# Talking-heads attention and a squared-ReLU FFN: rows loaded four to a partition, scores per head gathered by DMA into tiles of 10 queries by 12 heads, and the normalisation on GpSimd

## The chip, the cores and the metric

The kernel runs on one core of one Trainium2 chip. The metric is the device time of one execution in microseconds (us); less is better. Nanoseconds are marked ns.

In the profile's lines PE is TensorE's matmul, PEld its weight load, DVE is VectorE, ACT is ScalarE, POOL is GpSimd and SP is SyncE. L276 is line 276 of the kernel in question. "Span" is the length of the profiled execution. The "granted clock" (PEclk) is the share of TensorE's full clock that the profile records for a stretch, and a "run" of a transfer is a stretch of consecutive bytes in memory.

## The reference

There are 8 batches, 12 heads, 448 positions and a head size of 64. Scores are mixed across the heads before the softmax and once more after it ("talking heads"), and the attention's output goes through a squared-ReLU FFN (3584 tokens, 768 to 2048 to 768).

```python
scores = q @ k.T / 8                                   # per batch and head, 448 x 448
scores = einsum('bhij,hg->bgij', scores, w_pre)        # 12 heads -> 12 heads
attn   = exp(scores - max(scores))
attn   = attn / (sum(attn) + 1e-9)
attn   = einsum('bhij,hg->bgij', attn, w_post)         # 12 heads -> 12 heads
x      = (attn @ v) as (3584, 768)
h      = maximum(x @ w_in, 0)
out    = (h * h) @ w_out
```

q, k and v are drawn as normal numbers times 0.1, so the scores are small.

The mixing over heads is the awkward part. For each pair of positions it is a 12 by 12 matrix product. In these matmuls the contraction runs over partitions, so the heads have to lie on partitions, beside some queries: a block-diagonal matrix then mixes the heads of several queries in one matmul.

## The kernel before

It works in steps of 32 queries. 32 queries of 12 heads are 384 rows, which is three full tiles of 128 partitions. The 12 heads are split into 8 and 4 so that everything fits 128 partitions. That makes full use of the partitions, but each output tile needs two mix matmuls (heads 0 to 7, then 8 to 11), and the second mix again takes two.

```python
def load_rows(src, b, st, name):          # 128 positions on partitions: 256-byte runs (64 floats)
    ...
    nc.gpsimd.dma_start(out=t[0:n, :, :],
        in_=src[b, :, 128*st:128*st+n, :].rearrange("h s d -> s h d"))

def score_tile(s, t):                     # 3 per step; four 32-column matmuls each
    for r in range(4):
        nc.tensor.matmul(ps[32*r:32*r+32, 0:S], lhsT=ql[b%2][p][:, n, :], rhs=kts[(b, p)][:, :], ...)
    # copied to SBUF by ACT (t < 2) or DVE

def mix_O(s, u):                          # first mix: heads A, then heads B, into one bank
    nc.tensor.matmul(ps[:, 0:S], lhsT=preA[:, 0:128],  rhs=S_sb[(s, u)], start=True,  stop=False)
    nc.tensor.matmul(ps[:, 0:S], lhsT=preBA[u][:, :],  rhs=S_sb[(s, 2)], start=False, stop=True)
    softmax_tile(s, ps, u)
...                                       # (mix_AB and mix_BB do the third tile)
def softmax_tile(s, ps, t):
    nc.scalar.activation(out=e, in_=ps[:, 0:S], func=ACT.Exp, scale=SCALE, accum_out=sm)
    nc.vector.reciprocal(out=rc, in_=sm)
    nc.vector.tensor_scalar(out=d, in0=e, scalar1=rc, scalar2=1.0/S, op0=ALU.mult, op1=ALU.subtract)

def post(s, jb):                          # second mix, which also turns the tile: 3 per step,
    nc.tensor.matmul(ps[:, 0:384], lhsT=D_sb[(s, 2)][:, js], rhs=postBB, ...)
    for u in range(2):
        nc.tensor.matmul(ps[:, 192*u:192*u+192], lhsT=D_sb[(s, u)][:, js], rhs=postA, ...)
    nc.vector.tensor_copy(out=at[...], in_=ps[:, 0:384]...)
...                                       # (post_last does the 64 positions that remain)
```

The matmuls of attention times V (`ot_unit`) and of the FFN (`ffn1_unit`, `ffn2_unit`) are put in between as filler, so that TensorE has work while the softmax of a step runs.

The softmax here doesn't subtract the row's maximum and nothing guards it: scores larger than these inputs give would overflow.

Of the kernel before, what the change touches and what calls it, by code (L numbers as in the profile page):

```python
# [19 lines left out]
CH = 32  # L20
NCH = S // CH
HC = 16
NHC = S // HC
NHALF = 2
CPH = NCH // NHALF
SH = S // NHALF
SCALE = 1.0 / 8.0
ROWS = [128, 128, 128, 64]





# [3 lines left out]
def kernel(  # L37
# [18 lines left out]
    atbp = ctx.enter_context(tc.tile_pool(name="atbp", bufs=1))  # L56
# [7 lines left out]
    vfull = [[consts.tile([P, H, D], BF16, name=f"v{x}_{jb}") for jb in range(3)] for x in range(2)]  # L64

    vlast = [[consts.tile([P, H, D], BF16, name=f"vl{x}_{u}") for u in range(2)] for x in range(2)]

    def load_rows(src, b, st, name):
        n = ROWS[st]
        t = stage.tile([P, H, D], BF16, name=name, tag=name, bufs=4)  # L70
        nc.gpsimd.dma_start(out=t[0:n, :, :], in_=src[b, :, 128 * st:128 * st + n, :].rearrange("h s d -> s h d"))  # L71
        return t

    def load_qk(b):
        ks = [load_rows(k, b, st, "kst") for st in range(4)]
        qs = [load_rows(q, b, st, "qst") for st in range(4)]
        return qs, ks

    def load_v(b):
        x = b % 2  # L80
        for st in range(3):
            nc.gpsimd.dma_start(  # L82
                out=vfull[x][st][:, :, :], in_=v[b, :, 128 * st:128 * st + 128, :].rearrange("h s d -> s h d"))
        for u in range(2):
            nc.gpsimd.dma_start(
                out=vlast[x][u][64 * u:64 * u + 64, :, :], in_=v[b, :, 384:448, :].rearrange("h s d -> s h d"))

# [4 lines left out]
    def wcol(w, name, heads, eng):  # L92
        t = consts.tile([P, H], F32, name=name)
        for j, h in enumerate(heads):
            src = bass.AP(tensor=w.tensor, offset=w[h, 0:1].offset, ap=[[0, HC], [1, H]])
            eng.dma_start(out=t[HC * j:HC * j + HC, 0:H], in_=src)
        return t

    HA, HB = list(range(8)), [8, 9, 10, 11, 8, 9, 10, 11]
    cols = {  # L100
        "preA": wcol(w_pre, "preA_col", HA, nc.sync),
        "preB": wcol(w_pre, "preB_col", HB, nc.scalar),
        "postA": wcol(w_post, "postA_col", HA, nc.sync),
        "postB": wcol(w_post, "postB_col", HB, nc.scalar),
    }
    staged = {0: load_qk(0)}

    ql = [[consts.tile([P, NHC, 32], BF16, name=f"ql{x}_{p}") for p in range(NPAIR)] for x in range(2)]
    for p in range(NPAIR):
        nc.vector.memset(ql[0][p][:, :, :].rearrange("p a b -> p (a b)"), 0.0)  # L110
# [5 lines left out]
    istripe = consts.tile([P, HC], F32, name="istripe")  # L116
    nc.vector.tensor_reduce(out=istripe[:, :], in_=ident[:, :].rearrange("p (r i) -> p i r", i=HC),
                            axis=mybir.AxisListType.X, op=ALU.add)

    def cat(name):  # L120
        t = consts.tile([P, H, HC], BF16, name=name)
        nc.vector.tensor_tensor(out=t[:, :, :], in0=istripe[:, :].unsqueeze(1).to_broadcast([P, H, HC]),
                                in1=cols[name][:, :].unsqueeze(2).to_broadcast([P, H, HC]), op=ALU.mult)
        return t[:, :, :].rearrange("p g i -> p (g i)")

    preA = cat("preA")
    preB = cat("preB")

    preBA = [consts.tile([P, 128], BF16, name=f"preBA{u}") for u in range(2)]
    preBB = consts.tile([P, 128], BF16, name="preBB")  # L130
    nc.vector.memset(preBB[:, :], 0.0)
    for u in range(2):
        hs = slice(64 * u, 64 * u + 64)
        nc.vector.memset(preBA[u][:, :], 0.0)
        nc.vector.tensor_copy(out=preBA[u][hs, :], in_=preB[hs, 0:128])
        nc.vector.tensor_copy(out=preBB[hs, hs], in_=preB[hs, 128:192])
    postA = cat("postA")
    postB = cat("postB")
    postBB = consts.tile([P, 2 * H * HC], BF16, name="postBB")
    nc.vector.memset(postBB[:, :], 0.0)  # L140
    for u in range(2):
        hs = slice(64 * u, 64 * u + 64)
        nc.vector.tensor_copy(out=postBB[hs, 192 * u:192 * u + 192], in_=postB[hs, :])
# [6 lines left out]
    def late_loads():  # L150
        nc.gpsimd.dma_start(out=wpost_bf[:, :], in_=w_post[0:H, 0:H])
        load_v(0)
        staged[1] = load_qk(1)
        for x in range(2):
            for u in range(2):
                nc.gpsimd.memset(vlast[x][u][64 - 64 * u:128 - 64 * u, :, :].rearrange("p a b -> p (a b)"), 0.0)
        for p in range(NPAIR):
            nc.gpsimd.memset(ql[1][p][:, :, :].rearrange("p a b -> p (a b)"), 0.0)
        for c2 in range(NPAIR):
            nc.gpsimd.dma_start(out=w1[c2][:, :], in_=moe_w_in[c2 * 128:(c2 + 1) * 128, 0:DFF])  # L160
        for ft in range(FT):
            nc.gpsimd.dma_start(out=w2[ft][:, :], in_=moe_w_out[ft * 128:(ft + 1) * 128, 0:DMODEL])

    kts, bvecs, xts, h2ts, atbs = {}, {}, {}, {}, {}

# [11 lines left out]
    def transposes(ps, tiles, p):  # L177
        for st in range(4):
            n = ROWS[st]
            nc.tensor.transpose(ps[:, 128 * st:128 * st + n],  # L180
                                tiles[st][0:n, 2 * p:2 * p + 2, :].rearrange("s h d -> s (h d)"), ident[0:n, 0:n])

    def q_unit(b, p):
        ps = bank("qt_ps", BF16)
        transposes(ps, staged[b][0], p)
        for hh in range(2):
            r = slice(64 * hh, 64 * hh + 64)
            nc.vector.tensor_copy(out=ql[b % 2][p][r, :, 16 * hh:16 * hh + 16],
                                  in_=ps[r, 0:S].rearrange("p (n i) -> p n i", i=HC))

    def k_unit(b, p):
        ps = bank("kt_ps", BF16)
        transposes(ps, staged[b][1], p)
        kt_p = work.tile([P, S], BF16, name="kt_p", tag="kt", bufs=2 * NPAIR)
        nc.scalar.copy(out=kt_p[:, :], in_=ps[:, 0:S])
        kts[(b, p)] = kt_p

    def prologue_units(b):
        return [(400, lambda p=p, f=f: f(b, p)) for p in range(NPAIR) for f in (k_unit, q_unit)]

    def bias_unit(b):

        x = b % 2
        ps = bank("vs_ps")
        srcs = vfull[x] + [vlast[x][0]]
        for c2 in range(NPAIR):
            for jb in range(4):
                nc.tensor.matmul(ps[:, c2:c2 + 1], lhsT=srcs[jb][:, 2 * c2:2 * c2 + 2, :].rearrange("s h d -> s (h d)"),
                                 rhs=onescol[:, 0:1], start=(jb == 0), stop=(jb == 3))
        bv = work.tile([P, NPAIR], F32, name="bvec", tag="bvec", bufs=2)  # L210
        nc.vector.tensor_tensor(out=bv[:, :], in0=ps[:, 0:NPAIR], in1=cgblk[:, :], op=ALU.mult)
        bvecs[b] = bv

    def ot_unit(b, half, cp):

        x = b % 2
        at, at3 = atbs[(b, half)]
        ps = bank("ot_ps")
        for y in range(2):
            for jb in range(3):  # L220
                for hh in range(2):
                    g = 4 * cp + 2 * y + hh
                    nc.tensor.matmul(ps[64 * hh:64 * hh + 64, SH * y:SH * y + SH], lhsT=vfull[x][jb][:, g, :],  # L223
                                     rhs=at[:, jb, g, :], start=(y == 0 and jb == 0), stop=False,
                                     skip_group_check=True)
            for u in range(2):
                for hh in range(2):
                    g = 4 * cp + 2 * y + hh
                    dst = ps[64 * hh:64 * hh + 64, SH * y:SH * y + SH].rearrange("p (c u i) -> p u c i", u=2, i=HC)
                    nc.tensor.matmul(dst[:, u, :, :], lhsT=vlast[x][u][:, g, :], rhs=at3[:, g, :], start=False,  # L230
                                     stop=(u == 1), skip_group_check=True)
        for y in range(2):
            c2 = 2 * cp + y
            if (b, c2) not in xts:
                xts[(b, c2)] = ffnp.tile([P, S], BF16, name="xt", tag=f"xt{c2}", bufs=2)
            nc.scalar.activation(out=xts[(b, c2)][:, SH * half:SH * half + SH], in_=ps[:, SH * y:SH * y + SH],  # L236
                                 func=ACT.Identity, bias=bvecs[b][:, c2:c2 + 1], scale=1.0)
# [143 lines left out]
    with tc.manual_schedule(engines={PE}):  # L381
        for _, f in prologue_units(0):
            f()
# [85 lines left out]
```

## Time and profile before

| | before |
|---|---|
| time, median of 2 runs | 793.04 us (792.63 to 793.45) |
| span of the profiled execution | 791.2 us |
| first score matmul | 22.6 us |
| batch 0, first score matmul to that of batch 1 | 66.2 us |
| batch 1, likewise | 95.0 us |
| batches 2 to 6, likewise | 469.4 us, 93.9 each |
| batch 7 and the tail | 138.0 us |

The page of the kernel before, its busy row (busy time, share of the span, instructions), then the busy tenths of PE and its granted clock in 40 slices, the DMA packets, and the chain of work that ended last by engine:

```profile
PE 750.2 (95%) x7586; PEld 428.6 (54%) x7586; DVE 488.6 (62%) x1249; ACT 482.3 (61%) x1337; POOL 243.2 (31%) x271
...
PE   3689899999999999999999999999999999999997
...
PEclk9999999999999999999999999999999999999999
...
DMA packets 149336, 35.85 MB, mean 45 GB/s; under 512 B 139264, under 2 KB 148480, under 8 KB 149248
...
PE 85%; DVE 11%; DMA 2%; ACT 1%; issue 1%; ACTq 0%; DVEq 0%
...
L350 DVE CAST at<-at_ps 128x384 bf16<-128x384 f32 x336 | 184.0, 552 | 93.3 <-PE at_ps L348 90.4
L315 DVE TENSOR_SCALAR d_sb<-e_sb,rc 128x448 bf16<-128x448 f32 x336 | 171.9, 514 | 7.6
...
L327 PE MATMUL m_ps<-s_sb,preA 128*128 128x448 bf16 x224 | 80.3, 358 | 0.0
```

The group lines at the end read: line, engine, operation, output from inputs, shapes, how many, then the busy time and the mean ns of one, then the idle time of the engine before them and what ended it. TensorE is busy 95% of the span and over 90% in nearly every slice after the fourth. The normalisation, L315, takes 514 ns for 128x448 and 172 us of VectorE in all, but VectorE is busy only 62%.

The duration of a PE line is not its price: a matmul starts before the one before it has ended, and the starts tell the price. The timeline of PE before (start us, duration, engine, line, operation):

```profile
411.21 0.35 PE L327 MATMUL m_ps<-s_sb,preA 128*128 128x448 bf16 x1
411.40 0.35 PE L328 MATMUL m_ps<-s_sb,preBA_172 128*128 128x448 bf16 x1
411.59 0.33 PE L345 MATMUL at_ps<-postBB,d_sb 128*128 128x384 bf16 x1
411.75 0.33 PE L348 MATMUL at_ps<-postA,d_sb 128*128 128x192 bf16 x2
411.91 0.35 PE L245 MATMUL h_ps<-xt,w_0_191 128*128 128x448 bf16 x1
```

Each of these lasts 0.33 to 0.35 us by the record, but the next starts 0.19 us later after 448 columns, and 0.16 us later after 384 or twice 192. What counts here is how many columns are moved.

### The profile page before, as it was taken

The numbers are of one execution on the slowest core, as the hardware profiler recorded it, in microseconds if no ns is written. First come the engines' busy times: TensorE is split into PE (matmuls) and PEld (weight loads), VectorE is DVE, ScalarE is ACT, GpSimd is POOL, SyncE is SP. The second block draws the span as 40 slices with busy tenths as digits, with TensorE's granted clock in tenths as the row PEclk, the third lists the DMA queues.
The fourth block names the chain that finished last, engine by engine and source line by source line (L and its number), as shares of the span: only waits on it lengthen the run. The fifth ranks groups of instructions, "written<-read, shape, count | busy, mean of one in ns | idle before, by whom it ended". The sixth has DMA issues, their size and how long they took to land.

```text
span 791.2 us, 18851 instructions
## 1 busy us (share of the span) xinstructions
PE 750.2 (95%) x7586; PEld 428.6 (54%) x7586; DVE 488.6 (62%) x1249; ACT 482.3 (61%) x1337; POOL 243.2 (31%) x271
## 2 busy tenths in 40 slices
PE   3689899999999999999999999999999999999997
PEld 1245455555555555556555555555555565555654
DVE  2889868557685577656676576855766556555500
ACT  1477767547664577556766466754776457664641
POOL 6835255200570023700445005620053000420070
PEclk9999999999999999999999999999999999999999
DMA  9999967310690124911637106731060010001002
GB/s 111 74 206 158 66 41 51 42 46 7 41 72 31 41 16 28 70 42 31 41 25 57 51 12 41 50 42 46 7 42 1 32 41 2 2 12 50 12 1 70
DMA packets 149336, 35.85 MB, mean 45 GB/s; under 512 B 139264, under 2 KB 148480, under 8 KB 149248
## 3 DMA queue, kind: packets, MB, share of 16 engines
q0 software_dynamic: 140032, 23.60, 39.0%
q1 hardware_dynamic: 8704, 11.03, 4.2%
q8 instruction: 59, 0.97, 0.5%
q14 instruction: 29, 0.24, 0.1%
q10 hardware_dynamic: 512, 0.01, 0.1%
HBM read 47.21 MB, written 11.01 MB: 74 GB/s over the span
## 4 chain that ended last, share of the span: by engine, by line
PE 85%; DVE 11%; DMA 2%; ACT 1%; issue 1%; ACTq 0%; DVEq 0%
PE o_ps L263 19%; PE h_ps L245 18%; PE s_ps L291 8%; PE m_ps L327 6%; PE at_ps L345 6%; DVE d_sb L315 6%; PE at_ps L348 5%; PE m_ps L328 5%; PE mB_ps L321 4%; PE ot_ps L223 4%; DVE at L350 3%; PE mB_ps L305 2%; PE qt_ps L180 2%; PE kt_ps L180 2%; PE at_ps L359 2%; DMA postB_col<-in_w_post_dram 1%
## 5 line engine op out<-in xcount | busy, mean ns | idle before, releaser
L350 DVE CAST at<-at_ps 128x384 bf16<-128x384 f32 x336 | 184.0, 552 | 93.3 <-PE at_ps L348 90.4
L315 DVE TENSOR_SCALAR d_sb<-e_sb,rc 128x448 bf16<-128x448 f32 x336 | 171.9, 514 | 7.6
L295 ACT CAST s_sb<-s_ps 128x448 bf16<-128x448 f32 x224 | 108.2, 535 | 54.7 <-PE s_ps L291 52.8
L311 ACT ACTIVATE e_sb<-m_ps 128x448 f32<-128x448 f32 x224 | 121.1, 545 | 27.8 <-issue 23.9
L249 ACT ACTIVATE hr<-h_ps 128x448 f32<-128x448 f32 x128 | 69.7, 544 | 84.8 <-PE h_ps L245 84.0
L313 DVE RECIPROCAL rc<-sm 128x1 f32<-128x1 f32 x336 | 53.6, 160 | 100.5 <-ACT e_sb L311 99.6
L348 PE MATMUL at_ps<-postA,d_sb 128*128 128x192 bf16 x672 | 110.3, 246 | 0.0
L345 PE MATMUL at_ps<-postBB,d_sb 128*128 128x384 bf16 x336 | 109.9, 327 | 0.0
L297 DVE CAST s_sb<-s_ps 128x448 bf16<-128x448 f32 x112 | 69.8, 623 | 40.9 <-PE s_ps L291 40.9
L348 PEld LDWEIGHTS <-d_sb 128*128 128x128 bf16 x672 | 65.7, 98 | 40.8 <-issue 0.2
L327 PE MATMUL m_ps<-s_sb,preA 128*128 128x448 bf16 x224 | 80.3, 358 | 0.0
L269 ACT COPY osb<-o_ps 128x384 f32<-128x384 f32 x56 | 26.8, 479 | 71.4 <-PE o_ps L263 61.0
L311 ACT ACTIVATE e_sb<-mB_ps 128x448 f32<-128x448 f32 x112 | 63.1, 563 | 8.4 <-PE mB_ps L321 6.6
L359 PE MATMUL at_ps<-postA,d_sb 128*32 128x192 bf16 x448 | 37.3, 249 | 20.9 <-DVE d_sb L315 20.3
L82 POOL DMA_DIRECT2D v_0_79<-in_v_dram x4 | 4.3, 1066 | 152.0 <-PE ot_ps L230 151.2
L71 POOL DMA_DIRECT2D kst<-in_k_dram x32 | 32.1, 1012 | 51.9 <-PE kt_ps L180 43.6
L236 ACT ACTIVATE xt<-ot_ps,bvec 128x224 bf16<-128x224 f32 x96 | 37.7, 444 | 14.6 <-PE ot_ps L230 13.9
L311 ACT ACTIVATION_READ_ACCUMULATOR e_sb<-m_ps 128x1 f32 x224 | 46.1, 206 | 0.0
L245 PE MATMUL h_ps<-xt,w_0_191 128*128 128x448 bf16 x128 | 45.1, 353 | 0.0
L245 PE MATMUL h_ps<-xt,w_5_196 128*128 128x448 bf16 x128 | 45.1, 353 | 0.0
L245 PE MATMUL h_ps<-xt,w_2_193 128*128 128x448 bf16 x128 | 45.1, 352 | 0.0
L245 PE MATMUL h_ps<-xt,w_3_194 128*128 128x448 bf16 x128 | 45.1, 352 | 0.0
(602 smaller groups left out, 1921.4 us busy)
## 6 DMA issues: line engine op xcount, KB each, us to landing
out_dram<-osb SPq DMA_DIRECT2D x48, 192.0 KB, 1.9
kst<-in_k_dram POOLq DMA_DIRECT2D x24, 192.0 KB, 5.2
qst<-in_q_dram POOLq DMA_DIRECT2D x24, 192.0 KB, 5.0
out_dram<-osb SPq DMA_DIRECT2D x16, 96.0 KB, 2.2
kst<-in_k_dram POOLq DMA_DIRECT2D x8, 96.0 KB, 4.6
qst<-in_q_dram POOLq DMA_DIRECT2D x8, 96.0 KB, 3.9
v_0_76<-in_v_dram POOLq DMA_DIRECT2D x4, 192.0 KB, 4.7
v_1_77<-in_v_dram POOLq DMA_DIRECT2D x4, 192.0 KB, 6.0
```

The costliest lines, as they stand in the source:

```text
L245: nc.tensor.matmul(ps[:, 0:S], lhsT=w1[c2][:, ft * 128:(ft + 1) * 128], rhs=xts[(b, c2)][:, :], start=(c2 == 0), stop=(c2 == NPAIR - 1))
L249: nc.scalar.activation(out=hr[:, :], in_=ps[:, 0:S], func=ACT.Relu)
L263: nc.tensor.matmul(dst, lhsT=h2ts[(b, ft)][:, mt * 128:mt * 128 + ROWS[mt]], rhs=w2[ft][:, n2 * 384:(n2 + 1) * 384], start=(ft == 0), stop ...
L291: nc.tensor.matmul(ps[32 * r:32 * r + 32, 0:S], lhsT=ql[b % 2][p][:, n, :], rhs=kts[(b, p)][:, :], start=True, stop=True)
L295: nc.scalar.copy(out=sb[:, :], in_=ps[:, 0:S])
L297: nc.vector.tensor_copy(out=sb[:, :], in_=ps[:, 0:S])
L311: nc.scalar.activation(out=e[:, :], in_=ps[:, 0:S], func=ACT.Exp, scale=SCALE, accum_out=sm[:, 0:1])
L315: nc.vector.tensor_scalar(out=d[:, :], in0=e[:, :], scalar1=rc[:, 0:1], scalar2=1.0 / S, op0=ALU.mult, op1=ALU.subtract)
L327: nc.tensor.matmul(ps[:, 0:S], lhsT=preA[:, 0:128], rhs=S_sb[(s, u)][:, :], start=True, stop=False)
L345: nc.tensor.matmul(ps[:, 0:384], lhsT=D_sb[(s, 2)][:, js], rhs=postBB[:, :], start=True, stop=False, skip_group_check=True)
L348: nc.tensor.matmul(ps[:, 192 * u:192 * u + 192], lhsT=D_sb[(s, u)][:, js], rhs=postA, start=False, stop=True, skip_group_check=True)
L350: nc.vector.tensor_copy(out=at[:, jb, :, CH * cc:CH * cc + CH].rearrange("p g (u i) -> p g u i", u=2), in_=ps[:, 0:384].rearrange("p (u g ...
```

## The change

The intent is to do less on TensorE and to spread the rest:

- Four rows (positions) go to one partition, so that a load has runs of 1 KB instead of 256 bytes. 448 positions fill 112 partitions.
- Scores are made per head: 128 queries by 448 keys, contraction 64, so that two heads can use the two halves of the array's rows. They are copied to SBUF as blocks of 128 queries by 12 heads.
- A DMA on SyncE gathers 10 queries by 12 heads (120 rows, 105 KB) of such a block into one tile, six steps ahead.
- With all 12 heads of a query in one tile, the first mix is one matmul of 120 by 120, and the second is four of 120 columns.
- The normalisation goes from VectorE to GpSimd.
- A batch takes 45 steps of 10 queries instead of 14 of 32; the second mix lags the first by three steps.

```diff
-    nc.gpsimd.dma_start(out=t[0:n, :, :], in_=src[b, :, 128 * st:128 * st + n, :].rearrange("h s d -> s h d"))
+    nc.gpsimd.dma_start(out=t[0:PR, hs, :, :].rearrange("p h r d -> p h (r d)"),
+                        in_=src[b, hs, :, :].rearrange("h (p r) d -> p h (r d)", r=R))
 ...
+def score_burst(b, blk, pairs):
+    for p in pairs:
+        for hh in range(2):
+            rs = slice(64 * hh, 64 * hh + 64)
+            ps = bank("s_ps")
+            nc.tensor.matmul(ps[:, 0:S], lhsT=qTs[b][rs, p, BLK_START[blk]:BLK_START[blk] + P],
+                             rhs=kTs[b][rs, p, :], start=True, stop=True)
+    ...                                  # even heads copied by ACT, odd heads by DVE
+def gather(s):                           # AHEAD = 6 steps before its use
+    nc.sync.dma_start(out=g[0:n, :], in_=Sb[(b, blk)][x:x + n // H, :, :])
 ...
-    nc.tensor.matmul(ps[:, 0:S], lhsT=preA[:, 0:128], rhs=S_sb[(s, u)][:, :], start=True, stop=False)
-    nc.tensor.matmul(ps[:, 0:S], lhsT=preBA[u][:, :], rhs=S_sb[(s, 2)][:, :], start=False, stop=True)
+    nc.tensor.matmul(ps[0:n, 0:S], lhsT=pre[0:n, 0:n], rhs=Gs.pop(s)[0:n, :], start=True, stop=True)
 ...
-    nc.vector.tensor_scalar(out=d[:, :], in0=e[:, :], scalar1=rc[:, 0:1], scalar2=1.0 / S,
-                            op0=ALU.mult, op1=ALU.subtract)
+    nc.gpsimd.tensor_scalar(out=d[0:n, 0:S], in0=e[0:n, :], scalar1=rc[0:n, 0:1], scalar2=-1.0 / S,
+                            op0=ALU.mult, op1=ALU.add)
 ...
-    nc.tensor.matmul(ps[:, 0:384], lhsT=D_sb[(s, 2)][:, js], rhs=postBB[:, :], ...)
-    for u in range(2):
-        nc.tensor.matmul(ps[:, 192 * u:192 * u + 192], lhsT=D_sb[(s, u)][:, js], rhs=postA, ...)
+    for r in range(R):
+        nc.tensor.matmul(ps[:, RG * r:RG * r + RG], lhsT=d[0:n, PR * r:PR * r + P], rhs=post[0:n, :],
+                         start=True, stop=True)
 ...
+    vs[0] = load(v, 0, "v", 2)           # these loads stand before the step loop
+    for c2 in range(NPAIR):
+        nc.gpsimd.dma_start(out=w1[c2][:, :], ...)
+    kk = load(k, 1, "kst", 1); staged[1] = (load(q, 1, "qst", 1), kk)
+    for ft in range(FT):
+        nc.gpsimd.dma_start(out=w2[ft][:, :], ...)
```

The new kernel also turns q and k in 64-wide pairs, does attention times V in thirds of a batch, copies the FFN's output on VectorE instead of ScalarE, and puts the output's rows back in order when it stores them.

## The prediction

> **What bounds the kernel now.** PE. The page's busy row: PE 95% of 791 us, DVE 62%, ACT 61%, POOL 31%; the chain that ended last is 85% PE. In steady state a batch takes 98 to 99 us (stretches of that length hold 97 to 98 us of PE). Only the start (about 23 us until the first score matmul; first batch 95 us, 83 of PE) and the tail are bound otherwise. So the change is worth what it takes off PE's issue time per batch, unless another engine rises to that height.
>
> **PE per batch, from successive matmul starts in the timeline.** 448 moving columns take 0.19 us, full array or four 32-wide tiles; 192 columns 0.08; four transposes 0.40; a pair of 64-wide 224-column ones 0.095; a change of tile shape about 0.1.
> Before: 14 steps x 3.2 us (scores .58, mixes 1.14, post .98, last post .16, changes .3) = 44, transposes 4.8, AV 5.5, FFN 36.6, bias .6: sum 92, measured 98.5 (93%).
> After (estimates from those starts):
> - mix 45 x .19 = 8.6 (was 16)
> - unmix 45 x 4 x 120 columns, about .21 = 9.5 (was 16)
> - scores 48 x 448 as row pairs: 4.6 if pairs run together, 9.1 if not
> - transposes 96 of 112 columns in 64-wide pairs: 4.5 (9 if not together)
> - AV 4.7, FFN 36.6, bias 1, shape changes 4.8
>
> Sum 74 (up to 83). At before's 93%: 80 us a batch.
>
> **The others per batch.** ACT: 45 exponentials x (.545+.206), 24 score copies x .535, 16 relu x .544, 18 AV copies x about .38: 62 us. DVE: 45 unmix copies x about .65, 45 reciprocals x .16, 24 score copies x .62, 6 turn and 7 output copies: 59 us, little changed: the 0.51 us normalisation leaves (172 us in all), more copies come. POOL takes it: its two-input relu-square takes .95 us for 128x448. The Trainium skill, GPSIMD Engine Reference, Engine selection, calls one-input work "roughly line-rate"; I estimate 0.6 to 1.1 us for 120x448: 45 x .9 + 16 x .95 + 3 loads = about 60 us. No engine passes PE, but all reach 75 to 80% instead of 62, with a three-step lag and eight PSUM banks, and score bursts of four banks bunch ACT and DVE work.
>
> **DMA.** Packets under 512 B are 139264 of 149336 now, most of the loads' 39%; 1 KB runs shrink that fourfold, but past the start nothing waited on loads, so little time. New: 360 gathers of 107 KB in 896-byte rows on SP, beside output stores; a store lands in 1.9 us; issued six steps (about 10 us) ahead they should be hidden, except perhaps in batch 0 beside the weight loads.
>
> **Time.** Start 24 + batch 0 (no FFN, about 1.4 us a step) 65 + 7 x 80 + tail (last AV, FFN, store) 45 = 694; with 77 a batch 673. I say 685, range 640 to 740. Faster 0.93, within 2% 0.03, slower 0.04.
>
> **What will show it.** PE busy 600 to 650 us, still the top engine; batch period 75 to 83 us; normalisation under 1.1 us; score and transpose pairs starting within 0.02 us of each other; gathers landing in 2 to 4 us, mix hardly waiting on DMA; unmix matmuls about 53 ns apart.
>
> **What would make it wrong.** POOL's two-op instruction at 1.4 us or more: POOL sets the pace (over 80 us a batch). Pairs serialising: PE 83 us, total near 740. PE waiting for PSUM banks after each burst. Gathers late behind stores or weight loads. On the good side: PE at 98% of 74 us gives 645.

## More of the kernel before

Only TensorE's order is set by hand (`tc.manual_schedule(engines={PE})`); the order of instructions on the other engines is chosen by the framework's scheduler.

The windows view of the kernel before (columns: window, its length; busy us of PE, PEld, DVE, ACT, POOL with instructions in brackets; granted clock; DMA share; GB/s), for batch 0, batches 2 to 6, and the rest:

```profile
22.60:88.80 66.20, 56.63 (x624) 29.09 (x623) 56.72 (x146) 44.62 (x131) 39.91 (x53) 0.97 1.37 150
183.80:653.20 469.40, 461.76 (x4741) 266.57 (x4740) 303.24 (x766) 299.63 (x836) 131.78 (x137) 1.00 0.37 36
653.20:791.20 138.00, 130.89 (x1229) 75.31 (x1227) 58.41 (x154) 73.86 (x200) 29.86 (x32) 1.00 0.06 21
```

In steady state PE is busy 461.76 of 469.40 us, which is 98.4%. The kernel is bound by TensorE.

## The result, and the profile after

| | before | after |
|---|---|---|
| time, median of 2 runs | 793.04 us | 686.35 us (685.72 to 686.98) |
| ratio after to before (95%) | | 0.865 (0.863 to 0.868) |
| span of the profiled execution | 791.2 us | 684.8 us |
| PE busy | 750.2 us | 609.3 us |
| steady batch | 93.9 us | 75.55 us |

A ratio here is the mean time of one kernel's fast runs over the mean of the other's fast runs of the same rounds, so it is not quite the ratio of the medians quoted.

The kernel after takes 13.5% less time, and the number is the predicted one (685). The sum behind it is another matter, as will be seen.

The page of the kernel after, the same parts as shown of before:

```profile
PE 609.3 (89%) x6282; PEld 367.6 (54%) x6282; DVE 426.0 (62%) x1036; ACT 404.5 (59%) x1185; POOL 382.5 (56%) x545
...
PE   4207977899999999999999999999999999999897
...
PEclk9555898999999999999999999999999999999999
...
DMA packets 87959, 73.47 MB, mean 107 GB/s; under 512 B 5700, under 2 KB 84036, under 8 KB 87876
...
PE 71%; DMA 17%; DVE 6%; ACT 3%; issue 1%; POOL 1%; SPq 0%; DVEq 0%; ACTq 0%; POOLq 0%
...
L283 POOL TENSOR_SCALAR d<-e_sb,rc 120x448 bf16<-120x448 f32 x360 | 228.5, 638 | 202.7 <-DVE rc L281 200.6
L298 DVE CAST at<-at_ps 112x480 bf16<-112x480 f32 x360 | 231.4, 651 | 86.5 <-PE at_ps L296 83.3
...
L276 PE MATMUL m_ps<-G,pre 120*120 120x448 bf16 x360 | 135.8, 377 | 25.4 <-DMA G<-S 25.0
```

PE fell by 141 us, and it still is the busiest engine by far. But its busy row now begins 4, 2, 0, 7: there is a hole in the third slice (34 to 51 us), and the granted clock is about half in slices two to four. The hole comes back below.

The windows of the kernel after, for batch 0 (first to last mix), batches 2 to 6 (from the last mix of batch 1 to that of batch 6) and the rest:

```profile
27.10:104.40 77.30, 46.20 (x498) 26.43 (x499) 43.35 (x114) 40.01 (x123) 35.84 (x58) 0.72 0.88 155
188.80:566.50 377.70, 368.07 (x3927) 223.31 (x3925) 266.02 (x640) 250.67 (x740) 227.33 (x319) 1.00 0.59 107
566.50:684.80 118.30, 109.55 (x968) 66.26 (x966) 54.51 (x129) 58.25 (x166) 58.53 (x79) 0.98 0.31 64
```

In steady state PE is busy 368.07 of 377.70 us (97.5%). The next engine, VectorE, is at 70% there (266.02 us). Where the 106.4 us between the two traces went:

| stretch | before | after | difference |
|---|---|---|---|
| start, batch 0 and batch 1 | 183.8 us | 188.8 us | +5.0 |
| five steady batches | 469.4 us | 377.7 us | -91.7 |
| the rest | 138.0 us | 118.3 us | -19.7 |

(The borders are not the same event: the next batch's first score matmul before, the batch's last mix after. The lengths of the five batches do not depend on that; a few us can move between the first and the last row.) So the whole gain is in steady state and in the last batch, and the first two batches are, if anything, longer than before, although they too have the cheaper matmuls.

The timeline of PE after, in steady state:

```profile
404.17 0.35 PE L276 MATMUL m_ps<-G,pre 120*120 120x448 bf16 x1
404.36 0.37 PE L296 MATMUL at_ps<-post,d 120*128 120x120 bf16 x4
404.67 0.55 PE L251 MATMUL s_ps<-kT,qT 64*128 64x448 bf16 x4
405.15 1.47 PE L214 MATMUL o_ps<-w,h 128*128 128x384 bf16 x8
...
406.65 0.37 PE L296 MATMUL at_ps<-post,d 120*128 120x120 bf16 x4
406.86 0.33 PE L214 MATMUL o_ps<-w,h 128*128 128x384 bf16 x1
```

One mix is 0.19 us (404.17 to 404.36). Four second-mix matmuls are 0.21 us (406.65 to 406.86), 53 ns each. Four score matmuls take 0.48 us including the changes of shape (404.67 to 405.15); their own records start 0, 4, 199 and 203 ns after the first, that is two by two.

From such starts the saving on PE can be laid out, per batch. These are estimates from the starts of both traces; only some of them are tested below.

| work per batch | before, us | after, us |
|---|---|---|
| first mix | 14 x 1.14 = 16.0 | 45 x 0.19 = 8.6 |
| second mix | 14 x (0.98 + 0.16) = 16.0 | 45 x 0.21 = 9.5 |
| scores | 14 x 0.58 = 8.1 | 12 x 0.38 = 4.6 |
| q and k turned | 4.8 | 6 x 0.51 = 3.1 |
| shape changes | 14 x 0.3 = 4.2 | 4.8 |
| attention times V | 5.5 | 6 x 0.92 = 5.5 |
| FFN, bias | 37.2 | 37.6 |
| sum | 91.8 | 73.7 |

The sums differ by 18.1 us and the measured periods by 18.35.

Now the hole. The timeline of GpSimd after, around it (in brackets: idle time before the instruction, and what ended it):

```profile
32.35 0.53 POOL L334 DMA_DIRECT2D w<-in_moe_w_out_dram  x1 [2.15 <-DMA w<-in_moe_w_in_dram]
39.47 0.53 POOL L334 DMA_DIRECT2D w<-in_moe_w_out_dram  x1 [6.59 <-DMA kst<-in_k_dram]
...
52.35 0.53 POOL L334 DMA_DIRECT2D w<-in_moe_w_out_dram  x1 [0.41 <-DMA w<-in_moe_w_out_dram]
52.91 1.86 POOL L283 TENSOR_SCALAR d<-e_sb,rc 120x448 bf16<-120x448 f32 x3
```

and that of PE:

```profile
33.98 0.63 PE L276 MATMUL m_ps<-G,pre 120*120 120x448 bf16 x1
53.62 0.58 PE L296 MATMUL at_ps<-post,d 120*128 120x120 bf16 x4 [19.00 <-POOL d L283]
```

GpSimd also issues the loads. All loads of weights, of batch 0's v and of the next batch's q and k stand before the first normalisation in its instruction order, and from about 20 us on each issue waited for an earlier load to land. So the first normalisation ran at 52.9 us, although its input had been there since 28.6 us (the end of the first reciprocal, L281), and TensorE stood still for 19 us.

### The profile page after: what moved, and what is told of

It reads as the page before. It is cut to its first block, busy times and chain, and to the rows that moved or that the text cites. A ratio compares the mean times of both kernels' runs of the same rounds, so it can differ in the third digit from the quotient of the medians.

```text
span 684.8 us, 16963 instructions
## 1 busy us (share of the span) xinstructions
PE 609.3 (89%) x6282; PEld 367.6 (54%) x6282; DVE 426.0 (62%) x1036; ACT 404.5 (59%) x1185; POOL 382.5 (56%) x545
## 4 chain that ended last, share of the span: by engine, by line
PE 71%; DMA 17%; DVE 6%; ACT 3%; issue 1%; POOL 1%; SPq 0%; DVEq 0%; ACTq 0%; POOLq 0%
PE o_ps L214 20%; PE h_ps L187 18%; DMA G<-S 10%; PE at_ps L296 9%; PE m_ps L276 8%; PE ot_ps L170 6%; PE s_ps L251 5%; DMA qst<-in_q_dram 5%; PE tr_ps L144 3%; DVE at L298 3%; DVE S L258 2%; DMA out_dram<-osb 2%; ACT xt L178 1%; PE vs_ps L157 1%; DMA w<-in_moe_w_out_dram 1%
## 5 line engine op out<-in xcount | busy, mean ns | idle before, releaser
L283 POOL TENSOR_SCALAR d<-e_sb,rc 120x448 bf16<-120x448 f32 x360 | 228.5, 638 | 202.7 <-DVE rc L281 200.6
L298 DVE CAST at<-at_ps 112x480 bf16<-112x480 f32 x360 | 231.4, 651 | 86.5 <-PE at_ps L296 83.3
L279 ACT ACTIVATE e_sb<-m_ps 120x448 f32<-120x448 f32 x360 | 195.9, 547 | 146.3 <-PE m_ps L276 98.0
L187 PE MATMUL h_ps<-xt,w 128*128 128x448 bf16 x768 | 164.9, 354 | 0.0
L214 PE MATMUL o_ps<-w,h 128*128 128x384 bf16 (+1 forms) x1024 | 162.6, 327 | 0.0
L296 PE MATMUL at_ps<-post,d 120*128 120x120 bf16 (+1 forms) x1440 | 138.6, 220 | 22.6 <-POOL d L283 22.2
L276 PE MATMUL m_ps<-G,pre 120*120 120x448 bf16 x360 | 135.8, 377 | 25.4 <-DMA G<-S 25.0
L296 PEld LDWEIGHTS <-d 120*128 120x128 bf16 (+1 forms) x1440 | 104.5, 101 | 69.2 <-POOL d L283 26.7
L192 POOL TENSOR_TENSOR h<-hr 128x448 bf16<-128x448 f32 x128 | 119.2, 931 | 34.9 <-ACT hr L191 34.3
L258 DVE CAST S<-s_ps 128x448 bf16<-128x448 f32 x192 | 109.8, 614 | 3.3 <-DMA G<-S 1.6
L281 DVE RECIPROCAL rc<-sm 120x1 f32<-120x1 f32 x360 | 57.1, 159 | 81.6 <-ACT e_sb L279 78.3
L170 PE MATMUL ot_ps<-at,v 112*64 112x150 bf16 x1152 | 48.7, 236 | 12.3 <-DVE at L298 12.2
```

What stands on the lines that cost most here:

```text
L170: nc.tensor.matmul(ps[64 * hh:64 * hh + 64, TQ * y:TQ * y + TQ], lhsT=vs[b][0:PR, g, r, :], rhs=at[0:PR, r, g, :], start=(y == 0 and r == ...
L187: nc.tensor.matmul(ps[:, 0:S], lhsT=w1[c2][:, ft * 128:(ft + 1) * 128], rhs=xts[b][:, c2, :], start=(c2 == 0), stop=(c2 == NPAIR - 1))
L192: nc.gpsimd.tensor_tensor(out=h2[:, :], in0=hr[:, :], in1=hr[:, :], op=ALU.mult)
L214: nc.tensor.matmul(dst, lhsT=h2ts[(b, ft)][:, mt * 128:mt * 128 + ROWS[mt]], rhs=w2[ft][:, n2 * 384:(n2 + 1) * 384], start=(ft == 0), stop ...
L258: nc.vector.tensor_copy(out=sb[:, h, :], in_=ps[:, 0:S])
L276: nc.tensor.matmul(ps[0:n, 0:S], lhsT=pre[0:n, 0:n], rhs=Gs.pop(s)[0:n, :], start=True, stop=True)
```

## The experiments

The theory after reading the two traces was: in steady state TensorE's instruction stream sets the time, so the gain comes from fewer and paired matmuls; moving the normalisation gains nothing by itself, and it opens the hole at the start because GpSimd's loads stand before it. The rivals were: the gain comes from the relief of VectorE; the start is slow because of the weight traffic itself, not of GpSimd's order; the gain comes from the 1 KB runs. The expectations use letters for these theories; the text around them says what was at stake.

Overview (every kernel is the kernel after with one edit, but for the fourth, which is the kernel before with one edit):

| label | median us | ratio to before (95%) |
|---|---|---|
| e1_norm_vector | 686.86 | 0.866 (0.864 to 0.868) |
| e2_weights_late | 675.89 | 0.851 (0.848 to 0.855) |
| e3_norm_vector_12 | 675.46 | 0.853 (0.850 to 0.856) |
| e4_before_norm_pool | 829.93 | 1.046 (1.044 to 1.048) |
| e5_short_runs | 699.54 | 0.882 (0.879 to 0.885) |
| e6_ffn1_five_of_six | 668.24 | 0.843 (0.840 to 0.846) |
| e7_pairs_apart (median with its slow run) | 686.66 | 0.863 (0.860 to 0.865) |
| e8_weights_late_ordered | 664.25 | 0.838 (0.835 to 0.840) |
| e9_mix_twice | 737.13 | 0.928 (0.925 to 0.931) |
| e10_loads_retimed | 663.32 | 0.836 (0.834 to 0.838) |
| e11_ahead_three | 710.19 | 0.895 (0.893 to 0.897) |
| e12_pairs_same_rows | 713.09 | 0.899 (0.896 to 0.903) |

### Is the moved normalisation what gains? (e4, e1)

e4_before_norm_pool does that one part of the change in the kernel before:

```diff
-        nc.vector.tensor_scalar(out=d[:, :], in0=e[:, :], scalar1=rc[:, 0:1], scalar2=1.0 / S,
-                                op0=ALU.mult, op1=ALU.subtract)
+        nc.gpsimd.tensor_scalar(out=d[:, :], in0=e[:, :], scalar1=rc[:, 0:1], scalar2=-1.0 / S,
+                                op0=ALU.mult, op1=ALU.add)
```

> The kernel before, with only its normalisation moved to GpSimd. Theory A (the gain of the change is PE work taken out of each batch): no gain, 785 to 815 us (VectorE was not the limit; the start may lose some us behind load issues). Rival D (the gain of the change is mainly VectorE relieved of 172 us): 740 us or less.

It took 829.93 us, 4.6% more than before. VectorE's share fell to 40%, and nothing was gained by it: from 200 to 600 us PE was busy 388.0 of 400 us, against 393.6 in the kernel before. And the hole of the kernel after appeared here too. The timeline of GpSimd in e4:

```profile
62.94 0.53 POOL L162 DMA_DIRECT2D w<-in_moe_w_out_dram  x1 [0.40 <-DMA w<-in_moe_w_out_dram]
63.51 0.65 POOL L315 TENSOR_SCALAR d_sb<-e_sb,rc 128x448 bf16<-128x448 f32 x1
```

The waits view of e4 (who waited for whom: us in total, times, longest us):

```profile
PE at_ps L359 <- POOL d_sb L315: 55.7, 32, 34.7
```

The longest single wait of TensorE for the normalisation was 34.7 us, at the start, of the 38.9 us by which the traced span grew (830.1 against 791.2). That one part alone is thus a loss, and it is the start that loses. The expectation had the direction and the hole but was 15 us too low. That the relief of VectorE is the gain is refuted for the kernel before.

e1_norm_vector undoes the part in the kernel after:

```diff
-        nc.gpsimd.tensor_scalar(out=d[0:n, 0:S], in0=e[0:n, :], scalar1=rc[0:n, 0:1], scalar2=-1.0 / S,
+        nc.vector.tensor_scalar(out=d[0:n, 0:S], in0=e[0:n, :], scalar1=rc[0:n, 0:1], scalar2=-1.0 / S,
```

> The kernel after, with the normalisation (row 1/sum and minus 1/448) back on VectorE. Theory A (PE sets the steady batch of 75.5 us; the hole from 22 to 54 us is GpSimd's in-order queue, where the first normalisations wait behind the w2 load issues): the hole shrinks, the first unmix starts near 30 us instead of 53.6, but VectorE then has about 53 + 45 x 0.49 = 75 us of work per batch, as much as PE, so batches grow to 79 to 85 us; total 690 to 735. Rival B (the hole is DMA bandwidth: the gathers starve beside the weight loads, GpSimd's queue does not matter): first unmix stays near 50 us, total 715 to 760. Rival C (where the normalisation runs has no effect on the time): 686 within 1%.

It took 686.86 us: no difference from the kernel after within its spread, and below what my theory allowed. The total alone would speak for rival C of the expectation (no effect); the trace shows two effects. The zero is made of two parts. The first second-mix matmul came at 35.1 us instead of 53.6, batch 0 ended at 98.3 us instead of 104.4, and batch 1 took 80.6 us instead of 84.3; that is 9.9 us won. Then a steady batch took 77.3 us instead of 75.55 (mean of five) and the last one 72.9 instead of 70.1; that is 11.3 us lost. The windows view of e1, from 200 to 500 us:

```profile
200.00:500.00 300.00, 286.91 (x3024) 174.54 (x3024) 270.38 (x671) 192.53 (x569) 66.17 (x70) 0.99 0.59 107
```

VectorE is at 90% here (270.38 of 300), and still TensorE (286.91) sets the pace. In the new structure GpSimd's help is worth about 1.7 us a steady batch. I had expected a VectorE at 90% to hold TensorE back by much more.

### What does one us of TensorE's work cost? (e9, e6, e12, e7)

e9_mix_twice does each first mix twice, which changes no result and adds, at 0.19 us, 45 x 0.19 = 8.6 us of matmuls to a batch:

```diff
-        nc.tensor.matmul(ps[0:n, 0:S], lhsT=pre[0:n, 0:n], rhs=Gs.pop(s)[0:n, :], start=True, stop=True)
+        g = Gs.pop(s)
+        for _ in range(2):
+            nc.tensor.matmul(ps[0:n, 0:S], lhsT=pre[0:n, 0:n], rhs=g[0:n, :], start=True, stop=True)
```

> The kernel after with every mix matmul issued twice into the same bank (same result). It adds 45 x 0.19 = 8.6 us of PE to each batch and nothing to other engines. If PE's issue time sets the steady batch: 75.4 + 8.6 = 84 us, total 745 to 756 (batch 0 hides part of its share). If other engines or gathers leave PE slack in the steady batch, as the missing third of the gain in e6 hints: below 735.

It took 737.13 us, 8 us under the range expected of TensorE and above the rival's (below 735). The batches took 82.6 us, 7.1 us more than in the kernel after. The windows view of e9:

```profile
200.00:500.00 300.00, 296.08 (x3042) 180.95 (x3041) 196.37 (x469) 190.01 (x552) 174.00 (x240) 1.00 0.58 100
```

PE is now busy 98.7%. So more than four fifths of the added work reached the time, and the rest filled gaps in which TensorE had waited.

e6_ffn1_five_of_six takes PE work away. It leaves out one of six matmuls of each of the FFN's first products, 16 x 0.19 = 3.0 us a batch. Its output is wrong, which doesn't matter for the time.

```diff
-        for c2 in range(NPAIR):
+        for c2 in range(NPAIR - 1):
             nc.tensor.matmul(ps[:, 0:S], lhsT=w1[c2][:, ft * 128:(ft + 1) * 128], rhs=xts[b][:, c2, :],
-                             start=(c2 == 0), stop=(c2 == NPAIR - 1))
+                             start=(c2 == 0), stop=(c2 == NPAIR - 2))
```

> The kernel after with one of six matmuls of every FFN1 unit left out (a wrong result on purpose). It takes 16 x 0.19 = 3.0 us of PE out of every batch and nothing from the other engines. If PE's issue time sets the batch: batches of 72.3 us instead of 75.4, total 662 (658 to 667). If the other engines or PSUM banks set it: total above 678.

It took 668.24 us, 18 us less than the kernel after, where the full 3.0 us of eight batches would be 24; it just missed the range. A steady batch took 73.66 us (mean of five), 1.9 us less. The windows view of e6:

```profile
200.00:500.00 300.00, 287.19 (x3114) 175.46 (x3113) 215.17 (x520) 203.96 (x603) 187.57 (x263) 1.00 0.63 115
```

PE is idle 12.8 of 300 us here, which is 3.1 us of a batch, where it is 1.9 in the kernel after (9.63 us over five batches) and 1.1 in e9. TensorE sets the batch, but as its work gets shorter its waits for other engines grow, and they take part of what is saved. The last batch, which has no next batch's work beside it, did get the whole 3.0 us shorter (67.1 against 70.1).

e12_pairs_same_rows takes the pairing away. It puts all score matmuls on the upper 64 rows. The odd heads' scores are wrong. The run was still reported correct, presumably because the scores are so small that the tolerance does not see it.

```diff
-                rs = slice(64 * hh, 64 * hh + 64)
+                rs = slice(0, 64)
```

> The kernel after with all four score matmuls of a burst on the upper 64 rows of the array (the odd heads' scores are wrong on purpose); nothing else changes. e7 changed only the order and told nothing. If two matmuls on different row halves run side by side, this burst takes 4 x 0.19 us instead of 2 x 0.19: 96 bursts x 0.38 = 36 us more PE work, of which e9 paid five sixths: total 712 to 724. If the halves gain nothing: 686 within 0.5%.

It took 713.09 us, as expected of the pairing. The timeline of PE in e12:

```profile
401.59 0.93 PE L251 MATMUL s_ps<-kT,qT 64*128 64x448 bf16 x4
402.45 0.40 PE L276 MATMUL m_ps<-G,pre 120*120 120x448 bf16 x1
```

A burst of four takes 0.86 us here against 0.48 in the kernel after, and a steady batch 79.1 us against 75.55. In e12 the four records start 0, 200, 389 and 578 ns after the first, where in the kernel after they start two by two. The two heads on the two halves of the rows do run at once, and that is worth 27 us of the gain.

e7_pairs_apart had been meant to show the same by order alone, upper, upper, lower, lower instead of upper, lower, upper, lower:

```diff
-        for p in pairs:
-            for hh in range(2):
+        for hh in range(2):
+            for p in pairs:
```

> The kernel after with the four score matmuls of a burst in another order, upper rows, upper rows, lower rows, lower rows, so that only the middle two can run side by side. If pairs on different row halves run together, a burst takes 3 x 0.19 us instead of 2 x 0.19: 96 bursts x 0.19 = 18 us, total 700 to 707. If they don't run together anyway: 686 within 0.5%.

It took 686.66 us, no change: the burst took 0.49 us, and its records still start two by two (0, 7, 200 and 206 ns), although the first two were now both on the upper rows. In e12 two on the same rows start 0.19 to 0.20 us apart, so these records don't tell which matmuls ran side by side in e7. The order within the burst made no difference to the time; so e7 said nothing about the worth of the pairing, and e12 was needed.

### What makes the start slow? (e3, e2, e8, e10)

e3_norm_vector_12 puts only the first twelve normalisations on VectorE:

```diff
-        nc.gpsimd.tensor_scalar(out=d[0:n, 0:S], ...
+        norm_eng = nc.vector if s[0] == 0 and s[1] < 12 else nc.gpsimd
+        norm_eng.tensor_scalar(out=d[0:n, 0:S], ...
```

> The kernel after, with only the first 12 steps' normalisation on VectorE and all loads where they were. Theory A (GpSimd queue): first unmix near 30 us, no wait of PE for the normalisation of about 19 us, total 660 to 672. Rival B (DMA bandwidth): the gathers, not the normalisation, hold the first steps until the weights have landed near 50 us, total 680 to 688. Steady batches 75 to 76 us in both.

It took 675.46 us, between the two ranges. The hole at 34 us is gone, as the timeline of PE in e3 shows (compare 33.98 and 53.62 in the kernel after):

```profile
34.35 0.63 PE L276 MATMUL m_ps<-G,pre 120*120 120x448 bf16 x1
34.77 0.60 PE L297 MATMUL at_ps<-post,d 120*128 120x120 bf16 x4
...
59.33 0.58 PE L297 MATMUL at_ps<-post,d 120*128 120x120 bf16 x4 [5.00 <-POOL d L284]
```

Yet the end of batch 0 came only 10 us earlier (94.3 us). Of the 19 us of the hole about half came back in other places of batch 0. The last line shows one: after the twelfth step the normalisation is on GpSimd again, whose loads were still being issued until 58.6 us, and TensorE waited 5.00 us for it. Between 20 and 110 us TensorE's waits for GpSimd's normalisations fell from 20.2 us to 7.4; those for gathers were 20.3 us and are 18.1, so they are not what came back. In batch 0 TensorE's busy time rose from 46.20 to 50.61 us, at the same low granted clock (0.72 and 0.71). So the hole is GpSimd's order, with the load traffic left as it was, but batch 0 has a second limit behind it.

e2_weights_late moves the weight loads into the step loop of the program:

```diff
-        for c2 in range(NPAIR):
-            nc.gpsimd.dma_start(out=w1[c2][:, :], ...)          # likewise k, q of batch 1, and w2
         for i in range(len(steps) + LAG):
+            if i == 1:
+                kk = load(k, 1, "kst", 1); staged[1] = (load(q, 1, "qst", 1), kk)
+            if i in range(12, 36, 4):
+                nc.gpsimd.dma_start(out=w1[(i - 12) // 4][:, :], ...)
+            if i in range(34, 66, 2):
+                nc.gpsimd.dma_start(out=w2[(i - 34) // 2][:, :], ...)
```

> The kernel after, with the weight loads issued one at a time between the steps of batches 0 and 1 (w1 from step 12, w2 from step 34, the second batch's q and k at step 1). Theory A and rival B both expect the hole at 22 to 54 us to go: batch 0 ends near 80 us instead of 104, total 655 to 668. If later gathers starve beside the spread loads instead, the total stays above 675. Steady batches unchanged at 75 to 76 us.

It took 675.89 us, missed the range of both theories (655 to 668) and fell in the third outcome, above 675. The edit had not done what it says: only TensorE's order is binding, and the scheduler had moved most of GpSimd's loads forward again. The first second-mix matmul came at 29.3 us and batch 0 ended at 94.8 us; TensorE waited 24.3 us for gathers between 20 and 110 us.

e8_weights_late_ordered is the same with GpSimd's order set by hand too:

```diff
-    with tc.manual_schedule(engines={PE}):
+    with tc.manual_schedule(engines={PE, mybir.EngineType.Pool}):
```

> As e2 (weight loads between the steps), and GpSimd's instructions kept in the program's order, so that the loads really are issued one by one between the normalisations; in e2 the scheduler had moved most of them to the front again. If the 67 us that batch 0 still takes in e2 and e3 are gathers slowed by saturated DMA engines: batch 0 ends near 80 us instead of 94, total 655 to 664. If batch 0 is bound by something else (VectorE and ScalarE, or the cold PE clock): 668 to 676, as e2 and e3.

It took 664.25 us, at the upper edge of its first range and 22 us less than the kernel after. The timeline of PE in e8:

```profile
21.99 0.63 PE L276 MATMUL m_ps<-G,pre 120*120 120x448 bf16 x1 [4.96 <-DMA G<-S]
...
25.94 0.61 PE L296 MATMUL at_ps<-post,d 120*128 120x120 bf16 x4
```

The first mix started at 22.0 us instead of 27.1, the first second-mix matmul at 25.9, and batch 0 ended at 85.7 us instead of 104.4; batches 1 and later were as in the kernel after (84.4, then 75.0). So most of what the change lost at the start was the place of the loads in GpSimd's queue, and 19 of the 22 us are won in batch 0 and before it (the rest is a steady batch of 75.0 instead of 75.55 us). Of the 19, 14 lie in batch 0 and 5 before the first mix, for whose gather TensorE waited 4.96 us instead of 10.28. No normalisation had run by then, so these 5 us are probably the loads' traffic beside the gathers and not the order; e8 moves both and does not separate them. This beats both kernels.

e10_loads_retimed spreads the loads further, so that less traffic meets the gathers of batch 0: w1 from step 5 to 35 at every sixth step, w2 from step 37, v of batch 1 at step 44, q and k of batch 2 at step 50.

```diff
-            if i in range(12, 36, 4):
+            if i in range(5, 41, 6):                            # w1
-            if i in range(34, 66, 2):
+            if i in range(37, 69, 2):                           # w2
-                if t == 36 and b + 2 < B:                       # q, k two batches ahead
+                if (i == 50 or t == 36 and b > 0) and ...:
-                if t == 10 and b + 1 < B:                       # v one batch ahead
+                if (i == 44 or t == 10 and b > 0) and ...:
```

> As e8, with the loads of batches 0 and 1 spread further: w1 from step 5 every six steps, w2 from step 37 to 67, v of batch 1 at step 44, q and k of batch 2 at step 50. If batch 0's 64 us in e8 are still gathers slowed by loads: batch 0 ends near 78 us instead of 85.7, batch 1 takes 80 us instead of 84, total 650 to 660. If it is bound by VectorE, ScalarE or the cold PE clock: 661 to 667 as e8.

It took 663.32 us, the same as e8 within the spread: not in the range for loads that slow the gathers (650 to 660), but in the other (661 to 667), for a batch 0 bound by VectorE, ScalarE or a low granted clock. Batch 0 ended at 83.2 us, batch 1 took 84.2, and TensorE still waited 19.2 us for gathers before 110 us. What holds batch 0 at 62 to 64 us and batch 1 at 84 us, 9 more than a later one, stays open. The granted clock is the nearest candidate: from 35.0 to 49.7 us of e8 TensorE was busy 14.20 of 14.70 us at a granted clock of 0.50, and a mix there holds up the next start for 0.38 us instead of 0.19 (44.17 to 44.55). e8's batch 1 still has a mean clock of 0.91, the next batch 1.00. No run varied the clock by itself.

### Are the gathers far enough ahead? (e11)

```diff
-AHEAD = 6
+AHEAD = 3
```

> The kernel after with the gathers issued three steps ahead instead of six (three fewer buffers). Three steps are about 5 us; gathers that queue behind loads took 4 to 8 us on the chain. If six steps are needed to hide them: PE waits for gathers in every batch, 700 to 730. If three are enough in the steady batch: 686 to 692, with the loss in batch 0 only.

It took 710.19 us. The waits view of e11, from 190 to 600 us:

```profile
PE m_ps L276 <- DMA G<-S: 16.0, 9, 5.0
```

and of the kernel after, from 189 to 566 us:

```profile
PE m_ps L276 <- DMA G<-S: 1.7, 4, 0.8
```

With three steps of lead TensorE waits up to 5.0 us for a gather and a steady batch takes 79.6 us on average; with six the gathers are hidden in steady state. The DMA's traffic doubled (73.5 MB against 35.9), and that costs next to nothing there because of the lead.

### What are the 1 KB runs worth? (e5)

e5_short_runs loads 256-byte runs again, one position per run, and keeps everything else:

```diff
-            nc.gpsimd.dma_start(out=t[0:PR, hs, :, :].rearrange("p h r d -> p h (r d)"),
-                                in_=src[b, hs, :, :].rearrange("h (p r) d -> p h (r d)", r=R))
+            for x0 in range(R):
+                nc.gpsimd.dma_start(out=t[0:PR, hs, x0, :],
+                                    in_=src[b, hs, x0 * PR:x0 * PR + PR, :].rearrange("h p d -> p h d"))
-    out_rows = out.rearrange("(b p r) m -> b r p m", b=B, r=R)
+    out_rows = out.rearrange("(b r p) m -> b r p m", b=B, r=R)
```

> The kernel after with only the 1 KB runs undone: each partition takes rows p, 112+p, 224+p and 336+p, so the loads are in 256-byte runs and four DMAs for one, all else the same, output rows in plain order. Theory A (loads matter at the start, and by holding up gathers and GpSimd's queue, not in the steady batch): first mix some 8 us later, steady batches still 75 to 77 us, total 693 to 712. Rival E (the run length is a main part of the gain): over 725. Rival F (no effect): 686 within 0.5%.

It took 699.54 us, 13 us more than the kernel after. The page of e5:

```profile
DMA packets 186072, 73.48 MB, mean 105 GB/s; under 512 B 136068, under 2 KB 182148, under 8 KB 185988
```

The small packets are back (136068 under 512 bytes, against 5700), and the cost is all at the start: the first mix came at 36.4 us instead of 27.1, batch 0 ended at 120.0 us instead of 104.4, and from then on the batches were as in the kernel after (82.9, then 75.9 on average). But e5 changes two things: the runs are shorter, and four DMAs stand for one. The timelines of GpSimd and PE in e5:

```profile
1.32 8.54 POOL L72 DMA_DIRECT2D kst<-in_k_dram  x12 [0.87 <-POOLq L399]
...
19.27 0.96 PE L145 MATMUL tr_ps<-ident,kst 112*64 112x112 bf16 x16 [19.27 <-POOL ident masks.py:199]
```

and in the kernel after:

```profile
1.30 2.31 POOL L71 DMA_DIRECT2D kst<-in_k_dram  x3 [0.85 <-POOLq L398]
...
6.80 0.96 PE L144 MATMUL tr_ps<-ident,kst 112*64 112x112 bf16 x16 [6.80 <-POOL ident masks.py:199]
```

The issues of batch 0's k and q held GpSimd for 16.9 us instead of 4.4, and TensorE's first matmuls waited for `ident`, the identity matrix that GpSimd makes after them, and not for the data. The longest wait of TensorE for the normalisation grew too, from 19.00 to 21.55 us. So at least a large part of the 13 us is the time that GpSimd takes to issue four times the DMAs. The Trainium skill (DMA: Bandwidth & Descriptors, Specifications) puts the least transfer for line rate at 512 bytes; no run here tests the length of the run by itself. Runs and issues together are worth about an eighth of the gain of 107 us, and almost none of it in steady state.

## Why the prediction was right, and where it was not

The predicted 685 us met the measured 686.35 us, and that it came so close is partly luck: it was chosen between two sums, 694 and 673, and errors of opposite sign partly cancel in the terms below. Its mechanism, that TensorE's stream sets the time and loses about 18 us a batch, is what the runs showed: e9, e6 and e12 changed TensorE's work by +8.6, -3.0 and +4.6 us a batch (by count of columns) and the steady batch by +7.1, -1.9 and +3.5. But two sizes in the sum were wrong in opposite directions.

| term | predicted | measured | difference |
|---|---|---|---|
| start | 24 | 27.1 | +3.1 |
| batch 0 | 65 | 77.3 | +12.3 |
| seven more batches | 7 x 80 = 560 | 84.3 + 377.8 + 70.1 = 532.2 | -27.8 |
| tail | 45 | 48.2 | +3.2 |
| sum | 694 | 684.8 | -9.2 |

- **TensorE bounds the kernel, before and after.** Right: 98.4% and 97.5% in steady state.
- **The steady batch of before, "98 to 99 us" and "first batch 95 us".** Wrong, a misreading. The successive first score matmuls give 93.9 us for the steady batch and 66.2 us for batch 0; 95.0 is batch 1. So TensorE's efficiency was not 92/98.5 = 93%, it was 92/93.9 = 98%. This is the failed step: "at before's 93%: 80 us a batch". With the right factor the prediction's own 74 us gives 74/0.98 = 75.5 us, which is what was measured. This term was 28 us too large over seven batches: 22 in the five steady ones, and 10 in the last, which has no next batch's work beside it and took 70.1 us; batch 1 was 4 us over. The prediction had named this under "on the good side", with too little weight; its 645 us there does not follow from its own terms, which give 24 + 65 + 7 x 75.5 + 45 = 662.
- **TensorE's work after, 74 us.** Right as a sum. Turning q and k was over-sized (3.1 us, not 4.5) and attention times V under-sized (5.5, not 4.7). The mix, 53 ns per second-mix matmul and the pairs were right; e12 shows that the pairs count.
- **Batch 0, 65 us.** Wrong by 12 us. The prediction spoke of gathers beside weight loads; what stopped the batch was the place of the loads in GpSimd's queue, ahead of the normalisation that had newly moved there (19.00 us in one wait). The prediction costed the normalisation on GpSimd by its own duration and not by what stands before it. e4 shows the same in the old kernel, e8 takes it away. That batch 0 costs 62 to 64 us without the hole agrees with the 65.
- **The other engines.** Right that none passes TensorE, over-sized otherwise: in steady state VectorE is busy 53 us a batch (266.02/5; predicted 59), ScalarE 50 (62), GpSimd 45 (60). For ScalarE the prediction added the durations of instructions that overlap: the five groups of exp, its accumulator read, the score copies, the ReLU and the AV copies sum to 476.8 us, while the engine was busy 404.5. For GpSimd the normalisation took 0.638 us and not the 0.9 that the sum used.
- **The normalisation on GpSimd under 1.1 us.** Right (638 ns). But it gained next to nothing: 1.7 us a steady batch by e1, which the start took back.
- **1 KB runs, "little time".** Right: 13 us at most, nearly all at the start, and that includes the issuing of four DMAs for one in e5.
- **Gathers hidden in steady state, except perhaps in batch 0.** Right: 1.7 us of waits over five batches; e11 shows that it takes the six steps of lead.

What remains open: what limits batch 0 and batch 1 once the hole is gone (e10 did not move it), and how much each single piece of TensorE's saving gave. Only the price of a first mix (e9) and of the pairing (e12) was tested; the rest of that table is counting. The speed of TensorE's clock in batch 0 (a mean of 0.72 granted after, 0.97 before) was not varied by itself: in the kernel after it was 0.50 from 20 to 60 us, the stretch of the hole, but e8's batch 0, without the hole, still has 0.71, with PE busy 52 of 64 us.

## What to carry to other kernels

When TensorE is 98% busy, price a change by the starts of its matmuls, not their durations, and count columns moved: here that count was right to within 0.4 us a batch for the whole change, while of single pieces of work six to eight tenths reached the time (e9, e6, e12). Measure the period from one landmark to the same landmark of the next batch before dividing by it, because one wrong period cost more than all wrong durations together. When you move work to an engine that also issues loads, look at its instruction order: work that takes 0.64 us each stood 24 us behind loads that nothing needed yet, and giving these loads a later place gained another 22 us.

## What the Trainium skill lacked or had wrong

- GPSIMD Engine Reference, Engine selection, calls one-input elementwise work on GpSimd "roughly line-rate", while its Key points say that VectorE is about twice as fast for elementwise work; neither gives a figure for an instruction with two operations and a per-partition scalar. Here the same 128x448 instruction took 642 ns on GpSimd (e4) and 514 ns on VectorE (before), a factor of 1.25.
- DMA: Bandwidth & Descriptors, Rules for kernel authors, advises to issue a DMA early and wait late. It does not say what that costs when the issuing engine also computes. Here GpSimd's issues waited 1.9 us each for earlier loads to land, up to 6.59 us, and the normalisations behind them kept TensorE waiting 19.00 us (34.7 us in e4); with the loads issued later the whole kernel was 22 us faster (e8). I found no page that says what such a wait costs the compute instructions queued behind it.
- TensorE: Matmul & The Clock Gate, Back-to-back issue gap, gives about 81 ns per matmul for a sustained stream of weight load and matmul with 128 columns. Here matmuls of 120 columns, each with new weights, started 53 ns apart (0.21 us for four), so the page's figure is too high for a run of four.
- TensorEngine Tiling (Array Packing), Key Properties, says that a change of tiling mode drains TensorE, without a cost. Here a change costs about 0.1 us: from four second-mix matmuls to the score burst behind them 0.31 us pass, and 0.21 us where no change of shape follows.
